# Weight conversions of the second block started one unit earlier, unread products in every early pause, and shorter memsets

## The chip, the cores and the metric

The kernel runs on one core of one Trainium2 chip. The metric is the device time of one execution in microseconds (us). Five queues of instructions work side by side: TensorE (PE, matmuls; its weight loads are shown as PEld), VectorE (DVE), ScalarE (ACT), GpSimd (POOL), and SyncE (SP), which here only issues DMAs. TensorE runs at one of two clocks, 1.2 or 2.4 GHz; the profile shows the granted clock as a share of the higher one, 0.50 or 1.00.

## What is computed

Causal attention with a decay, and two feed-forward blocks behind it. Cut to what matters:

```python
scores = scale * np.matmul(q, k.transpose(0, 1, 3, 2))        # (4, 8, 576, 576)
cum = np.cumsum(np.log(np.clip(f, 0.0001, 1.0)), axis=-1)
scores = np.where(causal, -1e9, scores + cum[..., :, None] - cum[..., None, :])
attn = softmax(scores)                                         # sum + 1e-09
x = np.matmul(attn, v)  -> (2304, 512)
h = x @ moe_w_in;  g = np.maximum(0.01 * h, h);  y = g @ moe_w_out           # d_ff 2048
out = (silu(y @ moe2_w_gate) * (y @ moe2_w_val)) @ moe2_w_out                # d_ff 1536
```

The weights arrive as 64-bit floating point numbers; the kernel turns them into 32-bit ones itself.

## The kernel before, in words

The sequence of 576 positions is worked on in units (b, u): four batches b = 0 to 3, and in each a unit u = 0 of 320 queries in three row tiles and a unit u = 1 of 256 queries in two. So with 8 heads the attention of a unit is 24 or 16 steps. Unit (0, 0) is done in 32-bit matmuls (`attention_f32`), all others with operands split in two 16-bit parts: for each head the scores (PE), a custom VectorE operation with the decay and the mask, the exponential (ACT), the split into two halves (ACT and DVE, into `ph_ring`), and a DMA transpose that turns the probabilities for the product with V. Beside the attention of one unit run the matmuls of the first block (`moe_h`, `moe_y`) of the unit before it (`along`, line 1273). The second block runs after all attention, with its weights prepared by `prep_gv` and `prep_o2`.

The weights of the second block pass through `place` (line 879): a DMA of 512 KB of raw words into `stage`, three integer operations on VectorE that make 32-bit numbers (`to_f32`, line 538), a pass of ScalarE that finds the largest magnitude, and a DMA of 256 KB back to DRAM (`gate_val_dram`, or `out_dram` written from `wi_bytes` or `wo_bytes`; the name stands for the tensor `out2_dram`). There are 36 places: 24 for the gate and value weights (`stage_gv`) and 12 for the output weights (`stage_o2`). `along` takes one of them at each step t with t % every == 0; `every` is 2 in batches 2 and 3 and 0 in batch 1.

Nothing is issued as written. A planner (`Plan`) records every operation, works out dependences and due times, and simulates five queues in twelve rounds of list scheduling; the order with the shortest plan is emitted. So an edit in one place shifts the order elsewhere too. An operation recorded while `nc.behind` is set may not be planned ahead of the one it names; before, this holds for DMAs alone.

`emit` (line 353) also puts unread products into pauses of PE: 128x512 matmuls of zeroes out of `mask` into the last PSUM bank, `banks[-1]` (line 371), as many as fit in 0.9 of the planned pause at 216 ns each. Line 368 stops this at 30 us of the plan: `min(op.start, WARM)`.

In `decay` (line 578) VectorE forms the cumulated logarithms that the first heads need, while GpSimd writes constants: ones into four pieces of `wo_bytes`, and zeroes into the whole of the two buffers of `ph_ring` (six memsets of 128x768).

Of the kernel before, what the change touches and what calls it, by code (L numbers as in the profile page):

```python
# [20 lines left out]
P = 128  # L21
# [55 lines left out]
SLACK = 50e3  # L77
FILL = 0.9
FIRST = 2.5e3
WARM = 30e3  # L80
URG = 8


class Plan:
# [44 lines left out]
    def new(self, eng):  # L129
        op = Op()  # L130
        op.eng, op.calls, op.dur, op.succ, op.npred = eng, [], 0.0, [], 0
        op.reads, op.writes, op.bytes = [], [], 0
        op.urgent = self.urgent
        op.behind = None if self.urgent or eng != "SP" else self.behind
        return op

    def begin(self):
# [215 lines left out]
    def emit(self, rounds=12):  # L353
        self.link()
        self.dues()
        best = None
        for k in range(rounds):
            order = self.schedule(k == 0)
            end = max(op.end for op in order)
            if best is None or end < best[0]:  # L360
                best = (end, order, [(op.start, op.end) for op in self.ops])
            self.backward()
        for op, (a, b) in zip(self.ops, best[2]):
            op.start, op.end = a, b
        at = 0.0
        for op in best[1]:
            if op.eng == "PE":
                pause = min(op.start, WARM) - at + (FIRST if at == 0.0 else 0.0)
                for _ in range(int(max(0.0, pause) * FILL / (426.0 if at < COLD else 216.0))):
                    ps, w, x = self.filler  # L370
                    self.tensor.real.matmul(ps, lhsT=w, rhs=x, start=True, stop=True)
                at = op.end
            for fn, args, kw in op.calls:
                fn(*args, **kw)  # L374


class Ring:
# [5 lines left out]
    def next(self):  # L383
        self.n += 1
        return self.bufs[(self.n - 1) % len(self.bufs)]
# [21 lines left out]
def body(ctx, tc, qk, v, f, w_in, w_out, w_gate, w_val, w_out2, out):  # L407


    nc = Plan(tc.nc)  # L410
    B, H = qk.shape[:2]
# [6 lines left out]
    NF = DF // P  # L418
    NF2 = DF2 // P
# [3 lines left out]
    hw = P // 2  # L423


    UNITS = [(0, 320, (0, 1, 2)), (320, 256, (3, 4))]
    KEYS = [q0 + nq for q0, nq, _ in UNITS]
# [9 lines left out]
    NB2 = DF2 // FB2  # L437
# [32 lines left out]
    n = a_m.at  # L470
# [14 lines left out]
    NBK = [12, 18]  # L485
# [10 lines left out]
    n = KW[0][-1]  # L496
# [3 lines left out]
    n = 9 * P  # L500
# [77 lines left out]
    def decay():  # L578
        n0 = UNITS[0][1]
        scr = wo_t.t[:R, :]  # L580
        fr, one, cum = (scr[:, i * S:(i + 1) * S] for i in range(3))
        one = one[:, :n0]
# [15 lines left out]
        nc.gpsimd.partition_all_reduce(lib, lib, P, ABSMAX)  # L598
        nc.gpsimd.memset(mask, 0.0)
        nc.urgent = False  # L600

        nc.filler = (banks[-1], mask[:, :P], mask[:, :4 * P])
        nc.gpsimd.affine_select(out=mask[:, 4 * P:], in_=mask[:, 4 * P:], pattern=[[-1, P + hw]],
                                compare_op=ALU.is_ge, fill=NEG, base=0, channel_multiplier=1)
        csf = scr[:, 3 * S:3 * S + 4 * W].rearrange("r (a s) -> r a s", a=4)
        cs = csf.bitcast(F32R)

        for x in ph_ring.bufs:
            for a in range(0, NBK[1] * P, 6 * P):
                nc.gpsimd.memset(x[:, a:a + 6 * P], 0.0)  # L610
        for u, (q0, nq, _) in enumerate(UNITS):
            col, _, qc, kc = COLS[u]
            nc.gpsimd.memset(csf[:, :2, col + kc:col + kc + KEYS[u]], 1.0)
            nc.gpsimd.memset(csf[:, 2:, col + qc:col + qc + nq], 1.0)
        nc.scalar.copy(out=cum[:, :n0], in_=c0)
        nc.vector.tensor_tensor_scan(out=cum[:, n0:], data0=one[:, :S - n0], data1=fr[:, n0:],
                                     initial=c0[:, n0 - 1:n0], op0=ALU.mult, op1=ALU.add)
        for u, (q0, nq, _) in enumerate(UNITS):
            col, wd, qc, kc = COLS[u]
            n = KEYS[u]  # L620
# [267 lines left out]
    def stage_o2():  # L888
        for a in range(NF2):
            place(words(w_out2, NF2)[:, a:a + 1, :, :], o2d[a], am_o2[:, a:a + 1])  # L890
            yield

    def stage_gv(n):

        fs = slice(n * FB2, (n + 1) * FB2)
        ch = RAW // FB2
        nr = NC // ch
        for m, (w, s, i) in enumerate(((w_gate, s_g, i_g), (w_val, s_v2, i_v2))):
            am = sm(nr, "ami")
            for x in range(nr):  # L900
                place(words(w, NC)[:, x * ch:(x + 1) * ch, fs, :], gvd[2 * n + m, :, x * RAW:(x + 1) * RAW], am[:, x:x + 1])
                yield
            m1 = sm(1, "m1")
            nc.vector.tensor_reduce(out=m1, in_=am, axis=AX.X, op=ALU.max)

            scale_f32(s[:, n:n + 1], i[:, n:n + 1], m1, 13, "i")
# [351 lines left out]
    def chain(*gens):  # L1258
        for g in gens:
            yield from g  # L1260
# [12 lines left out]
    def along(at, mo, total, every=0):  # L1273

        cost = [0.0, 0.0]
        full = H * sum(KW[at[1]])
        for t, w in enumerate(at[0]):
            if every and t % every == 0:
                step(gv_places)
            cost[0] += w / full  # L1280
            while cost[1] < cost[0]:
                r = next(mo, None)
                if r is None:
                    break
                cost[1] += r / total
        run(mo)
# [21 lines left out]
    prev = (1, 0)  # L1308
    todo = [(b, u) for b in range(1, B) for u in range(2)][1:]
    gv_places = chain(*(stage_gv(n) for n in range(NB2)), stage_o2())  # L1310
    for b, u in todo:
        gs = []
        along((attention(b, u), u), chain(moe_h(*prev, gs), moe_y(*prev, gs)),
              12.0 * 2 * NF * UNITS[prev[1]][1], 2 if b > 1 else 0)
        prev = (b, u)
    run(gv_places)
    gs = []
# [74 lines left out]
```

## Time and profile before

| | us |
|---|---|
| median of 3 runs | 951.02 |
| lowest, highest run | 949.59, 953.21 |
| the profiled execution | 951.74 |
| its span | 949.7 |
| PE busy in the span | 919.4 (97%) |
| DVE busy | 801.7 (84%) |
| ACT busy | 679.7 (72%) |
| POOL busy | 46.4 (5%) |

A busy share near 100% says only that matmuls were in flight: a matmul at half clock, or an unread product, counts as busy like any other. So the busy shares are read together with the granted clock, and the idle stretches of PE together with what released it. Time runs from the start of the span; between the span and the time of the execution lie 2.0 us.

### The profile page before, as it was taken

The numbers are of one execution on the slowest core, as the hardware profiler recorded it, in microseconds if no ns is written. First come the engines' busy times: TensorE is split into PE (matmuls) and PEld (weight loads), VectorE is DVE, ScalarE is ACT, GpSimd is POOL, SyncE is SP. The second block draws the span as 40 slices with busy tenths as digits, with TensorE's granted clock in tenths as the row PEclk, the third lists the DMA queues.
The fourth block names the chain that finished last, engine by engine and source line by source line (L and its number), as shares of the span: only waits on it lengthen the run. The fifth ranks groups of instructions, "written<-read, shape, count | busy, mean of one in ns | idle before, by whom it ended". The sixth has DMA issues, their size and how long they took to land.

```text
span 949.7 us, 25231 instructions
## 1 busy us (share of the span) xinstructions
PE 919.4 (97%) x9951; PEld 787.6 (83%) x9951; DVE 801.7 (84%) x2052; ACT 679.7 (72%) x1673; POOL 46.4 (5%) x118
## 2 busy tenths in 40 slices
PE   8899999999998999998999999899999999999998
PEld 5567778877787777786777899889999999999997
DVE  7878999996789989889878999999587786958685
ACT  5857889996678988788786868767466574746462
POOL 5200000000000000100000000000000000000000
PEclk8979999999999999999999999999999999999999
DMA  7657995575899999989957243011001010010001
GB/s 225 186 162 232 265 204 148 122 173 136 169 236 237 272 255 249 260 226 320 273 112 185 97 131 116 23 52 41 24 24 36 13 35 24 25 35 2 25 2 46
DMA packets 162199, 128.22 MB, mean 135 GB/s; under 512 B 117232, under 2 KB 130544, under 8 KB 162048
## 3 DMA queue, kind: packets, MB, share of 16 engines
q1 hardware_dynamic: 162080, 126.61, 50.8%
q8 instruction: 78, 1.28, 0.5%
q14 instruction: 41, 0.34, 0.1%
HBM read 78.60 MB, written 19.63 MB: 103 GB/s over the span
## 4 chain that ended last, share of the span: by engine, by line
PE 56%; DVE 26%; DMA 9%; ACT 5%; issue 3%; SPq 1%; POOL 0%; DVEq 0%; ACTq 0%; POOLq 0%
PE bank L374 55%; DVE att_bytes L374 6%; DVE wi_bytes L374 5%; DVE g_bytes L374 4%; DVE stage L374 4%; DMA att_bytes<-att_bytes 4%; DVE wo_bytes L374 3%; ACT att_bytes L374 1%; DVE smalls L374 1%; DMA stage<-in_moe_w_val_dram 1%; DVE ta L374 1%; DVE tb L374 1%; DVE moe_bytes L374 1%; SPq L374 1%; ACT stage L374 1%
## 5 line engine op out<-in xcount | busy, mean ns | idle before, releaser
L374 PEld LDWEIGHTS <-att_bytes 128*128 128x128 f16 (+1 forms) x4062 | 234.8, 100 | 25.6 <-issue 21.2
L374 PE MATMUL bank<-g_bytes,wo_bytes 128*128 128x256 f16 (+2 forms) x1472 | 209.2, 297 | 0.8 <-DVE wo_bytes L374 0.5
L374 PE MATMUL bank<-moe_bytes,wi_bytes 128*128 128x256 f16 (+2 forms) x1472 | 205.8, 299 | 0.0
L374 ACT ACTIVATE att_bytes<-att_bytes,smalls 128x576 f32<-128x576 f32 (+12 forms) x308 | 173.9, 591 | 39.5 <-DVE smalls L374 31.3
L374 PEld LDWEIGHTS <-wi_bytes 128*128 128x128 f16 x2100 | 173.5, 98 | 32.9 <-issue 0.4
L374 PEld LDWEIGHTS <-wo_bytes 128*128 128x128 f16 x1344 | 127.0, 98 | 33.7 <-issue 2.9
L374 DVE TENSOR_TENSOR wi_bytes<-bank,wi_bytes 128x256 f32<-128x256 f32 x270 | 109.3, 419 | 42.4 <-PE bank L374 41.2
L374 PEld LDWEIGHTS <-g_bytes 128*128 128x128 f16 x1620 | 125.8, 98 | 11.6 <-issue 2.7
L374 ACT ACTIVATE wi_bytes<-wi_bytes,smalls 128x256 f32<-128x256 f32 (+2 forms) x129 | 69.9, 555 | 46.7 <-DVE wi_bytes L374 45.3
L374 PE MATMUL bank<-wi_bytes,att_bytes 128*128 128x128 f16 x1680 | 98.7, 219 | 0.7 <-DVE wi_bytes L374 0.7
L374 DVE SCALAR_TENSOR_TENSOR att_bytes<-att_bytes,smalls 128x576 f16<-128x576 f32 (+5 forms) x148 | 86.2, 615 | 5.6 <-ACT att_bytes L374 5.5
L374 PE MATMUL bank<-stage,att_bytes 128*128 128x128 f16 (+1 forms) x1389 | 86.7, 221 | 2.6 <-DVE wi_bytes L374 2.4
L374 DVE CUSTOM_DVE_ANT_0 att_bytes<-bank,att_bytes 128x320 f32<-128x320 f32 (+5 forms) x160 | 67.8, 443 | 14.5 <-PE bank L374 14.0
L374 ACT COPY wi_bytes<-bank 128x256 f32<-128x256 f32 x108 | 38.3, 364 | 55.6 <-PE bank L374 50.2
L374 PE MATMUL bank<-tb 68*128 68x256 f32 (+3 forms) x168 | 62.3, 381 | 3.6 <-ACT att_bytes L374 2.2
L374 PE MATMUL bank<-att_bytes 128*64 128x256 f16 (+3 forms) x804 | 48.5, 257 | 12.2 <-DMA att_bytes<-att_bytes 9.9
L374 POOL PARTITION_ALL_REDUCE smalls<-smalls x47 | 24.2, 518 | 691.5 <-DVE smalls L374 689.7
L374 DVE TENSOR_TENSOR g_bytes<-moe_bytes,g_bytes 128x320 f16<-128x320 f32 (+1 forms) x80 | 45.1, 567 | 14.0 <-ACT g_bytes L374 13.5
L374 ACT ACTIVATE wi_bytes<-wo_bytes 128x256 bf16<-128x256 f32 x108 | 44.0, 410 | 17.9 <-DVE wo_bytes L374 17.8
L374 PE MATMUL bank<-wo_bytes,g_bytes 128*128 128x256 f16 x432 | 54.9, 273 | 0.0
L374 PE MATMUL bank<-ta 128*128 128x256 f32 (+3 forms) x168 | 51.2, 315 | 0.0
L374 ACT ACTIVATE moe_bytes<-bank 128x320 f32<-128x320 f32 (+1 forms) x80 | 39.3, 492 | 11.4 <-PE bank L374 10.4
(123 smaller groups left out, 1425.7 us busy)
## 6 DMA issues: line engine op xcount, KB each, us to landing
stage<-in_moe_w_out_dram SPq DMA_DIRECT2D x28, 512.0 KB
att_bytes<-in_qk_dram SPq DMA_DIRECT2D x32, 416.0 KB
stage<-in_moe_w_in_dram SPq DMA_DIRECT2D x16, 512.0 KB
att_bytes<-in_qk_dram SPq DMA_DIRECT2D x24, 320.0 KB
stage<-in_moe_w_gate_dram SPq DMA_DIRECT2D x12, 512.0 KB
stage<-in_moe_w_val_dram SPq DMA_DIRECT2D x12, 512.0 KB
stage<-gate_val_dram SPq DMA_DIRECT2D x12, 512.0 KB
ta<-y_dram SPq DMA_DIRECT2D x18, 256.0 KB
```

What stands on the lines that cost most here:

```text
L374: fn(*args, **kw)
```

## The change

Four edits. The places of the second block start one unit earlier, in unit (1, 1), at an unchanged rate: 36 places over 72 steps is one in two steps (`rate`), so that they end after 16 of the 24 steps of unit (3, 0); before they began in (2, 0) and ended in (3, 1). The unread products are put into every planned pause until the first real product that writes the last bank, not only up to 30 us. The zeroes for `ph_ring` are written only to the halves of four blocks that no later operation writes before they are read. The ones in `wo_bytes` are written by ScalarE, as copies, and not ahead of the first scan of `decay`.

```diff
-WARM = 30e3
-        op.behind = None if self.urgent or eng != "SP" else self.behind
+        op.behind = None if self.urgent and eng == "SP" else self.behind
...
-        at = 0.0
+        at, bank = 0.0, self.filler[0].tensor.name
         for op in best[1]:
             if op.eng == "PE":
-                pause = min(op.start, WARM) - at + (FIRST if at == 0.0 else 0.0)
+                if bank in (w[0] for w in op.writes):
+                    bank = None
+                pause = op.start - at + (FIRST if at == 0.0 else 0.0) if bank else 0.0
...
+        scan = next(o for o in reversed(nc.ops) if o.eng == "DVE")
...
         for x in ph_ring.bufs:
-            for a in range(0, NBK[1] * P, 6 * P):
-                nc.gpsimd.memset(x[:, a:a + 6 * P], 0.0)
+            for i in (3, 8):
+                nc.gpsimd.memset(x.rearrange("p (n k) -> p n k", k=P)[:, i::9, hw:], 0.0)
+        nc.behind = scan
         for u, (q0, nq, _) in enumerate(UNITS):
             col, _, qc, kc = COLS[u]
-            nc.gpsimd.memset(csf[:, :2, col + kc:col + kc + KEYS[u]], 1.0)
-            nc.gpsimd.memset(csf[:, 2:, col + qc:col + qc + nq], 1.0)
+            for a, c, n in ((0, kc, KEYS[u]), (2, qc, nq)):
+                x = csf[:, a:a + 2, col + c:col + c + n]
+                nc.scalar.copy(out=x, in_=one[:, :1].unsqueeze(2).to_broadcast(x.shape))
+        nc.behind = None
...
-            if every and t % every == 0:
+            for _ in range(int((t + 1) * every) - int(t * every)):
                 step(gv_places)
...
+    rate = (4 * NB2 + NF2) / (sum(H * len(UNITS[u][2]) for _, u in todo) - 24)
     for b, u in todo:
...
-              12.0 * 2 * NF * UNITS[prev[1]][1], 2 if b > 1 else 0)
+              12.0 * 2 * NF * UNITS[prev[1]][1], rate)
```

In the changed file the unread products stand on line 372 and all other instructions on line 375, where before they stand on 371 and 374.

**ScalarE in `decay`.** The rows after the first copy on ScalarE. Before:

```order
L374 COPY wo_bytes<-wo_bytes 32x320
L374 ACTIVATE wo_bytes<-wo_bytes 32x320
L374 ACTIVATE wo_bytes<-wo_bytes 32x256
L374 ACTIVATE wo_bytes<-wo_bytes 32x320
L374 ACTIVATE wo_bytes<-wo_bytes 32x256
L374 ACTIVATE att_bytes,smalls<-att_bytes,smalls 128x320
```

With the change:

```order
L375 COPY wo_bytes<-wo_bytes 32x320
L375 COPY wo_bytes<-wo_bytes 32x2x576
L375 COPY wo_bytes<-wo_bytes 32x2x320 x2
L375 COPY wo_bytes<-wo_bytes 32x2x256
L375 ACTIVATE wo_bytes<-wo_bytes 32x320 x2
L375 ACTIVATE att_bytes,smalls<-att_bytes,smalls 128x320
```

Four copies now stand ahead of the first exponential (128x320); two of the smaller activations have moved behind the first nine exponentials. In the same place GpSimd's list has lost four memsets of `wo_bytes`, and its six memsets of 128x768 have become four of 128x2x64.

**PE at the end of `attention_f32`.** The scores of the last head (from `att_bytes` alone) and the diagonal products that turn its probabilities (`g_bytes,att_bytes`). Before:

```order
L374 MATMUL bank_68<-att_bytes 128x192
L374 MATMUL bank_69<-att_bytes 128x320
L374 MATMUL bank_67<-att_bytes 128x64
L374 MATMUL bank_73<-g_bytes,att_bytes 128x128 x2
L374 MATMUL bank_73<-g_bytes,att_bytes 64x128
L374 MATMUL bank_72<-g_bytes,att_bytes 128x128
```

With the change:

```order
L375 MATMUL bank_69<-att_bytes 128x320
L372 LDWEIGHTS att_bytes
L372 MATMUL bank_74<-att_bytes 128x512
...
L375 MATMUL bank_73<-g_bytes,att_bytes 128x128 x2
L375 MATMUL bank_73<-g_bytes,att_bytes 64x128
L375 MATMUL bank_71<-g_bytes,att_bytes 64x128
```

Sixteen unread products (the two rows on line 372, sixteen times) now stand between the last scores and the diagonal products; before, none. In the whole program there are 63 of them instead of 41; four stand ahead of the first product of the first block, the rest in other pauses of `attention_f32`.

**SP at the end of unit (3, 0).** The last DMA transposes of the unit (128x12x128), and the raw loads of the output weights (`in_moe_w_out_dram`). Before:

```order
L374 DMA_TRANSPOSE att_bytes<-att_bytes 128x12x128
L374 DMA stage<-in_moe_w_out_dram 128x1024
L374 DMA att_bytes<-in_qk_dram 128x832
L374 DMA_TRANSPOSE att_bytes<-att_bytes 128x12x128
L374 DMA tb_84<-cum_dram 4x832
L374 DMA out_dram<-wo_bytes 128x512
L374 DMA att_bytes<-in_qk_dram 128x832
L374 DMA stage<-in_moe_w_out_dram 128x1024
L374 DMA y_dram<-moe_bytes 128x2x256 x2
```

With the change:

```order
L375 DMA_TRANSPOSE att_bytes<-att_bytes 128x12x128
L375 DMA tb_84<-cum_dram 4x832
L375 DMA att_bytes<-in_qk_dram 128x832
L375 DMA tb_85<-cum_dram 4x832
L375 DMA_TRANSPOSE att_bytes<-att_bytes 128x12x128 x2
L375 DMA tb_84<-cum_dram 4x832
L375 DMA att_bytes<-in_qk_dram 128x832 x2
L375 DMA y_dram<-moe_bytes 128x2x256 x2
```

No raw load and no store of converted weights stands beside the last three transposes any more. In exchange, eight raw loads now stand among the eight transposes of unit (1, 1), where there were none.

## Rows read from the trace of the kernel before

**Rows 1.** The page: PE's granted clock in 40 slices, tenths.
```profile
PEclk8979999999999999999999999999999999999999
```

**Rows 2.** Windows: stretch, busy us of PE, PEld, DVE, ACT, POOL; clock; DMA share; GB/s.
```profile
12.00:19.00 7.00, 7.00 (x26) 4.83 (x25) 5.95 (x25) 4.50 (x21) 2.54 (x6) 0.51 0.94 293
48.00:58.00 10.00, 10.00 (x34) 6.62 (x35) 8.11 (x21) 5.11 (x16) 0.80 (x2) 0.50 0.61 176
450.40:455.10 4.70, 4.70 (x34) 3.73 (x34) 4.70 (x9) 4.49 (x11) 0.15 (x1) 0.50 1.07 411
```

**Rows 3.** Timeline, PE's idle time: start, us, operation, [idle before it, and its releaser].
```profile
11.06 1.40 PE L374 MATMUL bank<-att_bytes 66*128 66x320 f32 x6 [2.35 <-DVE smalls L374]
47.97 3.62 PE L374 MATMUL bank<-g_bytes,att_bytes 128*128 128x128 f32 x12 [3.37 <-POOL g_bytes L374]
450.40 1.76 PE L374 MATMUL bank<-att_bytes 128*64 128x64 f16 x23 [3.35 <-DMA att_bytes<-att_bytes]
617.76 0.83 PE L374 MATMUL bank<-stage,att_bytes 128*128 128x128 f16 x12 [1.90 <-DVE wi_bytes L374]
```

**Rows 4.** Groups by shape on DVE and POOL, 0 to 12 us: count | busy, mean ns.
```profile
L374 DVE TENSOR_SCALAR wo_bytes<-wo_bytes 32x320 fp32r<-32x320 f32 x1 | 2.6, 2623 | 0.3 <-ACT wo_bytes L374 0.3
L374 DVE TENSOR_SCALAR wo_bytes<-wo_bytes 32x576 fp32r<-32x576 f32 x1 | 1.1, 1059 | 0.0
L374 DVE TENSOR_SCALAR wo_bytes<-wo_bytes 32x576 f32<-32x576 f32 x1 | 0.5, 500 | 0.9 <-DMA wo_bytes<-in_f_dram 0.9
L374 POOL MEMSET att_bytes<- 128x768 f16 x6 | 4.6, 808 | 0.0
```

**Rows 5.** Timeline of ACT in the first 12 us.
```profile
3.34 0.68 ACT L374 ACTIVATE wo_bytes<-wo_bytes 32x576 f32<-32x576 f32 x1 [1.26 <-DVE wo_bytes L374]
5.45 0.44 ACT L374 COPY wo_bytes<-wo_bytes 32x320 f32<-32x320 f32 x1
9.96 0.47 ACT L374 ACTIVATE wo_bytes<-wo_bytes 32x320 fp32r<-32x320 f32 x1 [3.27 <-DVE wo_bytes L374]
11.04 0.56 ACT L374 ACTIVATE att_bytes<-att_bytes,smalls 128x320 f32<-128x320 f32 x1
```

**Rows 6.** Timeline of PE: diagonal products of the first heads.
```profile
14.70 3.56 PE L374 MATMUL bank<-g_bytes,att_bytes 128*128 128x128 f32 x12
```

**Rows 7.** Windows as in Rows 2: behind the second fall, to 200 us, and unit (1, 1).
```profile
48.00:62.00 14.00, 14.00 (x46) 9.27 (x47) 9.43 (x24) 7.13 (x20) 0.80 (x2) 0.57 0.61 181
80.00:200.00 120.00, 117.27 (x878) 93.92 (x877) 116.30 (x319) 108.41 (x256) 2.64 (x11) 1.00 0.79 196
200.00:260.00 60.00, 60.00 (x490) 44.56 (x490) 44.81 (x123) 44.98 (x97) 2.17 (x7) 1.00 0.64 141
```

**Rows 8.** The chain that ended last, pieces of DMA: start, us, transfer.
```profile
68.69 4.57 DMA stage<-in_moe_w_in_dram
443.09 7.27 DMA att_bytes<-att_bytes
```

**Rows 9.** The tile stage: count, duration ns min/median/max, first and last start.
```profile
L374 DVE TENSOR_SCALAR stage<-stage x68: 390/422/606, 14.9 to 482.8; 128x512 int32<-128x512 int32 x68
L374 DVE SCALAR_TENSOR_TENSOR stage<-stage x68: 651/689/769, 15.4 to 485.8; 128x512 int32<-128x512 int32 x68
L374 DVE SCALAR_TENSOR_TENSOR wi_bytes<-stage x34: 675/686/777, 17.2 to 468.2; 128x512 int32<-128x512 int32 x34
```

**Rows 10.** Timeline of PE: what waits at the ends of other units.
```profile
197.56 1.00 PE L374 MATMUL bank<-att_bytes 128*64 128x64 f16 x23 [1.08 <-DMA att_bytes<-att_bytes]
322.75 1.00 PE L374 MATMUL bank<-att_bytes 128*64 128x64 f16 x23 [1.58 <-DMA att_bytes<-att_bytes]
390.93 1.56 PE L374 MATMUL bank<-att_bytes 128*64 128x256 f16 x29 [1.30 <-DMA att_bytes<-att_bytes]
```

**Rows 11.** Timeline of SP around the end of unit (3, 0).
```profile
441.98 0.53 SPq L374 DMA_DIRECT2D stage<-in_moe_w_out_dram  x1
447.37 1.01 SPq L374 DMA_DIRECT2D stage<-in_moe_w_out_dram  x1
```

## The prediction

> **What bounds the kernel now.** I read PE first. It is busy for 919.4 of 949.7 us, so all its idle time together is 30 us, and no change of order can be worth more than that, except through the clock. So the second view is the granted clock: in 40 slices it is under 90% in the first and the third only [rows 1]. Finer windows show three stretches at half clock: 12 to 19 us (0.51), 48 to 58 us (0.50) and 450.4 to 455.1 us (0.50), with PE busy throughout [rows 2]. Work done at half clock takes twice its time, so these three cost about 3.4, 5.0 and 2.35 us. The third view is PE's idle time and its releasers: in front of each of these stretches PE had waited 2.35, 3.37 and 3.35 us, while the longest wait that no fall followed is 1.90 us [rows 3]. The first wait ends on VectorE, the second on GpSimd, the third on a DMA transpose. These three pauses and what they do to the clock are 9.07 + 10.75 = 19.8 us; the change touches all three. Behind the second fall VectorE is the late engine: from 80 to 200 us it is busy for 116.3 of 120 us, PE for 117.3 [rows 7]. So there is hardly slack there to lose a gain in, nor to find another.
>
> **The first pause: memsets.** Before the first heads VectorE runs two TENSOR_SCALAR in 3.68 us, and the smaller one (320 columns) takes 2.62 us against 1.06 us for 576 columns; an earlier one of 576 columns took 0.50 us [rows 4]. What runs beside them is GpSimd's six memsets of 0.81 us, 4.6 us in all. With the change these are four memsets of a sixth of the size, and the four of `wo_bytes` are gone, so GpSimd should be done before VectorE comes to this pair. By the 0.50 us row the pair then takes 0.8 us (0.50, and 320/576 of it), at worst the 1.06 us that the larger one still took, twice: 2.1 us. VectorE is 2.9 (1.6) us earlier, and PE's wait of 2.35 us, which is for VectorE to read the first head's scores, goes, or shrinks to 0.75 us. Then the clock has no reason to fall at 12 us. Together that would be up to 2.35 + 3.4 = 5.75 us.
>
> The Trainium skill, "SBUF — State Buffer", section "SBUF: two separate sides", has a rule for this: VectorE (in a mode that takes both ports) and GpSimd share one pair of ports, whoever starts first holds it for a whole instruction, and the other blocks. By that rule each of the pair waits for one memset at most, 2 x 0.81 us; the change would then give back 1.6 us and not 2.9. The trace does not agree with it in size, since 2.62 us is longer than a memset and the 0.50 us row together.
>
> But the ones of `wo_bytes` are now ScalarE's, four copies of 1152, 640, 640 and 512 columns ahead of the first exponential. By the slope between 0.44 us for 320 columns and 0.68 us for 576 [rows 5] these are 1.2, 0.75, 0.75 and 0.6 us, 3.3 us. ScalarE is free at 5.89 us, ends the copies at 9.2, two activations of 0.47 us later stands at 10.1, and so starts its exponentials 0.9 us earlier than the 11.04 us of before, not 2.4. The cover of VectorE's and PE's gain is thus short: the first diagonal products need the exponentials. I count the 0.9 us, and that the diagonal products of the first heads take 1.8 us at full clock in place of 3.56 [rows 6], and the like of it once more, 0.65 us, for the scores between: 3.3 us. Bounds: 0.9 us (the clock falls all the same) and 5.75 us.
>
> **The second pause: unread products.** Sixteen of them at 0.22 us are 3.5 us in a pause of 3.37 us, and they hold the clock if the pause is where the plan has it. Then the stretch from 48 to 58 us runs at full clock: 5.0 us. VectorE can follow, being idle for 4.6 of the 14 us from 48 to 62 [rows 7], mostly in waits for PE. Their cost: 0.1 us of overrun and 0.9 us for the four ahead of the first block, if no pause is there. 4.0 us. Bounds: 5.0 us, and a loss of 1.0 us if the pause has moved.
>
> What is late next are the raw loads of the first block's weights, whose landing stands in the chain at 68.69 us with 4.57 us [rows 8]. They are issued when VectorE frees a buffer of `stage`, so they move with it; I keep all 7.3 us for the likeliest case and price their loss as a rival.
>
> **The conversions.** A place costs VectorE 0.42 + 0.69 + 0.69 = 1.80 us [rows 9], 512 KB in and 256 KB out; ScalarE's pass and SP's two issues move with it. 36 places stay 36 places. What changes is what they stand beside. At the end of unit (3, 0) the last transpose is issued at 443.09 us, between raw loads at 441.98 and 447.37 [rows 11], and lands 7.27 us later [rows 8]; PE waits 3.35 us for it and then works 4.7 us at half clock. With the change no raw load stands there. Left is what the end of a unit without conversions shows, 1.08 us [rows 10]. 3.35 + 2.35 - 1.08 = 4.6 us gained; bounds 0 (the transposes are late anyway) and 5.7.
>
> In exchange eight places come into unit (1, 1). There PE is not idle at all, and VectorE for 60 - 44.8 = 15.2 us [rows 7]; eight places are 14.4 us, so they just fit. The end of (1, 1) will look like the end of a unit with conversions: 1.58 and 1.30 us of waiting, without a fall [rows 10]. I take 1.5 us, after the second, which is the same kind of unit (the 1.30 us, and 0.2 us within it); bounds 0 and 5.7 us (it goes as at 450 us).
>
> **Sum.** 3.3 + 4.0 + 4.6 - 1.5 = 10.4 us. From the profiled execution of 951.74 us that is 941.3; the median of the runs is 0.7 us lower, so 940.6 us against 951.02.
>
> **Rivals.**
> A, the start is given back. VectorE and the raw loads bound 60 to 200 us, and the loads land when DRAM delivers them. For it: the chain goes through them and through VectorE, not PE. Against it: from 48 to 62 us the DMA share is only 0.61 [rows 7]. Only the conversions stay: 951.0 - 3.1 = 947.9 us, within 0.5%.
> B, the change does not do what it says at the second pause: the sixteen products end before the real wait does, or stand ahead of it, and the clock falls as before. For it: the plan's pauses are a model's. Against it: plan and trace have the pause in the same place. 3.3 + 4.6 - 1.5 - 1.0 = 5.4 us: 945.6 us.
> C, slower. VectorE is full in (1, 1): 44.8 + 14.4 = 59.2 of 60 us. Then the probabilities of its four pairs of heads are split late, each pair's last transpose lands late among raw loads, and PE waits as at 450 us, 3.35 us and 2.35 us of half clock, 5.7 us each time. It decides from the third of these on: 4 are 22.8 us, 3 are 17.1, against 3.3 + 4.0 + 4.6 = 11.9 us gained. With three, 951.0 + 5.2 = 956.2 us. For it: VectorE's 15.2 us of idle time lie in waits, not in a block. Against it: units (2, 0) and (2, 1) carry the same rate, and each shows one such wait at its end, of 1.58 and 1.30 us, with no fall.
>
> **How the numbers follow.** The forecast gets 0.60, A 0.18, B 0.12, C 0.10. The predicted time is that of the forecast, 940.6 us. A measurement of this kernel can tell about 0.5%, 4.8 us, from no change. The range reaches down to 935.0 us (5.75 + 5.0 + 4.6 = 15.4 us with nothing lost in (1, 1) is 935.6) and up over B and A to 950.0 us; what is left out is C and the ends of the forecast. The forecast's own range is 935 to 946. Faster by over 0.5% (below 946.3): 0.71, being the forecast and most of B; within: 0.19; slower: 0.10.
>
> **What the changed profile would show.** Right: two TENSOR_SCALAR of `wo_bytes` near 0.3 and 0.5 us; no wait of PE over 2 us before 60 us, and a granted clock of 1.00 throughout; the diagonal products of 47.97 us some 3 us earlier; the wait at the end of (3, 0) near 1 us; VectorE nearly full from 195 to 255 us and PE's waits there under 2 us in all. Wrong: a stretch at 0.50 left between 40 and 60 us (B); the start earlier but the first product behind 197 us not (A); two or more waits of over 2 us in (1, 1) (C). The forecast falls altogether if the new order, which twelve rounds of planning make anew, has put a wait of over 2 us where none was before, since each brings its half clock with it.

## The result, and the profile after

The changed kernel takes 941.91 us (median of 7 runs, 938.83 to 946.57) against 951.02 us before: a ratio of 0.9908 with a 95% interval of 0.9881 to 0.9934, or 8.7 us (6.3 to 11.3). 940.6 us had been forecast, within 935 to 950. The profiled execution took 940.95 us, its span 939.2. The page, PE's row and the granted clock in 40 slices, to be held against [rows 1]:

```profile
span 939.2 us, 25235 instructions
PE 915.0 (97%) x9969; PEld 784.4 (84%) x9973; DVE 798.9 (85%) x2052; ACT 681.6 (73%) x1677; POOL 40.6 (4%) x112
PEclk9999999999999999999999999999999999999999
```

The three stretches of [rows 2], and those of [rows 7] that answer, in windows (stretch, its length, busy us and instructions of PE, PEld, DVE, ACT and POOL; granted clock; DMA share; GB/s):

```profile
12.00:19.00 7.00, 6.63 (x41) 4.54 (x41) 6.85 (x20) 6.10 (x27) 4.01 (x8) 1.00 1.07 266
48.00:58.00 10.00, 9.84 (x46) 6.69 (x46) 9.87 (x25) 8.56 (x22) 0.00 (x0) 1.00 0.47 140
450.40:455.10 4.70, 4.70 (x37) 3.40 (x35) 3.73 (x10) 4.48 (x12) 0.00 (x0) 1.00 0.99 188
80.00:200.00 120.00, 115.99 (x894) 93.28 (x893) 114.91 (x324) 106.67 (x252) 2.90 (x12) 1.00 0.83 192
200.00:260.00 60.00, 58.52 (x473) 42.89 (x472) 53.70 (x151) 46.31 (x108) 3.74 (x9) 1.00 0.91 208
```

All three falls are gone (0.51, 0.50 and 0.50 before), and the same 10 us from 48 on hold 46 matmuls (three of them unread) where 34 stood. One fall is new, too short to show in 40 slices: about 3 us at half clock from 607.7 us on, which cost 1.6 us (its window stands in the last section). What PE lost for it is in the last two rows: it waits 4.0 us between 80 and 200 us (2.7 before), and 1.5 between 200 and 260, where it had not waited at all. Its waits that answer to [rows 3] and [rows 10], and the new ones (timeline: start, us, operation, count, in brackets the idle time ahead and what ended it):

```profile
42.96 4.08 PE L375 MATMUL bank<-g_bytes,att_bytes 128*128 128x128 f32 x24 [1.23 <-POOL g_bytes L375]
127.36 1.56 PE L375 MATMUL bank<-att_bytes 128*64 128x256 f16 x29 [2.01 <-DMA att_bytes<-att_bytes]
261.75 1.56 PE L375 MATMUL bank<-att_bytes 128*64 128x256 f16 x29 [1.67 <-DMA att_bytes<-att_bytes]
307.61 0.36 PE L375 MATMUL bank<-tb 68*128 68x256 f32 x1 [2.11 <-DMA tb<-cum_dram]
441.93 0.44 PE L375 MATMUL bank<-tb 68*128 68x448 f32 x1 [0.83 <-issue]
444.38 1.03 PE L375 MATMUL bank<-att_bytes 128*64 128x64 f16 x24
606.71 0.83 PE L375 MATMUL bank<-stage,att_bytes 128*128 128x128 f16 x12 [1.90 <-DVE wi_bytes L375]
```

No wait stands near 11 us any more, and the second pause is down from 3.37 to 1.23 us. At the end of unit (3, 0) the wait of 3.35 us for the last transpose is gone altogether: the products that read it, at 444.38 us, wait for nothing. The 0.83 us at 441.93 stand ahead of another operation and end on nothing that the profile shows. The conversions (the tile `stage`, as in [rows 9]) now end with unit (3, 0)'s second third:

```profile
L375 DVE TENSOR_SCALAR stage<-stage x68: 378/422/515, 12.4 to 430.6; 128x512 int32<-128x512 int32 x68
```

**What PE loses, stretch by stretch.** For every profile I summed, over windows of 1 us, PE's idle time and the part of its busy time that half clock took (busy time, times one less the granted clock). What is left of the span is work at full clock: 906 to 908 us, and 5 to 7 us more with the unread products in all early pauses. All sums are from one execution each, and some of these lie at the edge of their kernel's times: a_nomem and a_norate are the fastest of ten and twelve, f_only, a_norate48 and after48 the slowest of eleven, six and six. So a row shows where an execution lost time; by how much two kernels differ is told by the medians.

| profile of | 0-65 | 65-200 | 200-430 | 430-455 | 455-625 | 625-end | work | span |
|---|---|---|---|---|---|---|---|---|
| before | 16.7 | 2.7 | 6.1 | 6.5 | 6.4 | 3.8 | 907.3 | 949.7 |
| changed | 3.6 | 4.0 | 8.6 | 0.8 | 5.6 | 3.3 | 913.3 | 939.2 |
| f_only | 7.0 | 3.1 | 5.6 | 6.8 | 10.1 | 3.1 | 912.7 | 948.4 |
| m_only | 12.1 | 1.5 | 7.8 | 7.8 | 7.8 | 4.3 | 906.1 | 947.4 |
| r_only | 17.3 | 2.3 | 11.0 | 0.8 | 6.3 | 3.8 | 908.1 | 949.5 |
| a_nofill | 12.4 | 2.0 | 11.2 | 0.5 | 6.7 | 3.1 | 906.8 | 942.8 |
| a_nomem | 3.7 | 2.3 | 9.3 | 1.1 | 4.7 | 3.1 | 912.9 | 937.0 |
| a_norate | 3.0 | 2.6 | 9.0 | 7.7 | 7.7 | 3.4 | 911.4 | 945.0 |
| a_norate_b | 2.6 | 3.7 | 9.9 | 6.0 | 8.8 | 4.2 | 912.7 | 947.7 |
| a_norate48 | 5.3 | 4.7 | 7.3 | 7.4 | 6.3 | 4.0 | 913.5 | 948.6 |
| after48 | 5.4 | 3.2 | 15.3 | 1.2 | 4.5 | 3.1 | 912.8 | 945.5 |
| a_spread | 3.2 | 4.9 | 4.9 | 2.6 | 11.5 | 3.7 | 912.8 | 943.5 |
| b_quarter | 15.3 | 4.7 | 3.4 | 5.9 | 7.0 | 3.8 | 906.2 | 946.1 |
| cs_only | 12.2 | 2.4 | 11.9 | 6.0 | 8.0 | 3.1 | 905.7 | 949.3 |

From before to the changed kernel: 13.1 us less at the start, less 6.0 us of unread work; 1.3 us more from 65 to 200; 2.5 more from 200 to 430; 5.7 less from 430 to 455; 1.3 less behind. That is 10.3 of the 10.5 us between the spans.

### The profile page after: what moved, and what is told of

Read it like the earlier page. It is cut to its first block, busy times and chain, and to the rows that moved or that the text cites. A ratio compares the mean times of both kernels' runs of the same rounds, so it can differ in the third digit from the quotient of the medians.

```text
span 939.2 us, 25235 instructions
## 1 busy us (share of the span) xinstructions
PE 915.0 (97%) x9969; PEld 784.4 (84%) x9973; DVE 798.9 (85%) x2052; ACT 681.6 (73%) x1677; POOL 40.6 (4%) x112
## 3 DMA queue, kind: packets, MB, share of 16 engines
q8 instruction: 78, 1.28, 0.6%
## 4 chain that ended last, share of the span: by engine, by line
PE 57%; DVE 25%; DMA 8%; ACT 5%; issue 3%; SPq 1%; POOL 1%; ACTq 0%; DVEq 0%; POOLq 0%
PE bank L375 56%; DVE att_bytes L375 6%; DVE wi_bytes L375 5%; DMA att_bytes<-att_bytes 4%; DVE stage L375 4%; DVE g_bytes L375 4%; DVE wo_bytes L375 2%; ACT att_bytes L375 2%; DVE smalls L375 1%; PE bank L372 1%; DMA stage<-in_moe_w_gate_dram 1%; DVE tb L375 1%; DVE moe_bytes L375 1%; DVE ta L375 1%; SPq L375 1%
## 5 line engine op out<-in xcount | busy, mean ns | idle before, releaser
L375 PE MATMUL bank<-moe_bytes,wi_bytes 128*128 128x256 f16 (+2 forms) x1472 | 202.7, 297 | 1.2 <-DVE moe_bytes L375 1.1
L375 ACT ACTIVATE att_bytes<-att_bytes,smalls 128x320 f32<-128x320 f32 (+11 forms) x308 | 174.2, 591 | 37.3 <-DVE smalls L375 23.7
L375 DVE CUSTOM_DVE_ANT_0 att_bytes<-bank,att_bytes 128x320 f32<-128x320 f32 (+6 forms) x160 | 67.8, 443 | 9.4 <-PE bank L375 9.2
L375 DVE TENSOR_TENSOR g_bytes<-moe_bytes,g_bytes 128x320 f16<-128x320 f32 (+1 forms) x80 | 45.0, 566 | 11.6 <-ACT g_bytes L375 11.2
L375 ACT CAST ta<-att_bytes 128x832 fp32r<-128x832 f32 (+1 forms) x56 | 45.2, 807 | 3.2 <-PE bank L375 2.7
```

## The experiments

Times of a kernel are medians; one execution differs from another of the same kernel by some 5 us either way, so a profile shows where time lies and the ratio says what an edit is worth. Where a gain in us is given, it is the ratio's distance from 1, times 950.9 us.

**Each edit alone, and all without one.** The edits were told apart by their pieces of the diff: f, the unread products; m, the short memsets with the ones of `wo_bytes` on ScalarE; r, the spread conversions. An m or an r gives the planner other work and so another order everywhere; f changes no order, since the unread products go in after the planning, and the instructions of DVE, ACT and SP are the same with and without it.

f_only, the kernel before with this alone:

```diff
-                pause = min(op.start, WARM) - at + (FIRST if at == 0.0 else 0.0)
+                if bank in (w[0] for w in op.writes):
+                    bank = None
+                pause = op.start - at + (FIRST if at == 0.0 else 0.0) if bank else 0.0
```

> The kernel before with the unread products in all early pauses alone. Theory (each term stands for itself): the first pause stays as in [rows 3], 2.35 us behind VectorE, and its fall to 0.51 from 12 to 19 us too; the fall from 48 to 58 us is gone, and the diagonal products of 47.97 us run at full clock. 4 to 5 us are gained: about 946.5 us, and the end of (3, 0) still shows 3.35 us and a fall. Rival (the gain is given back behind the pause, where VectorE is full from 80 to 200 us): the fall is gone, the first store of y_dram (140.0 us before) is under 2 us earlier, and the time is 950 us or over.

946.33 us, ratio 0.9955 (0.9932 to 0.9977): 4.3 us. Windows of its profile, the first fall and where the second was:

```profile
12.00:19.00 7.00, 7.00 (x26) 4.64 (x25) 6.22 (x26) 4.49 (x21) 2.53 (x6) 0.55 0.98 298
48.00:58.00 10.00, 10.00 (x53) 6.87 (x52) 9.88 (x25) 7.48 (x22) 0.95 (x3) 1.00 0.69 204
```

The first fall stays, behind a pause of 2.05 us, and the second is gone, as the theory had it. Of the 9.7 us that the start loses less, 5.4 are paid as unread work.

m_only, the memsets alone:

```diff
-            for a in range(0, NBK[1] * P, 6 * P):
-                nc.gpsimd.memset(x[:, a:a + 6 * P], 0.0)
+            for i in (3, 8):
+                nc.gpsimd.memset(x.rearrange("p (n k) -> p n k", k=P)[:, i::9, hw:], 0.0)
...
-            nc.gpsimd.memset(csf[:, :2, col + kc:col + kc + KEYS[u]], 1.0)
+                nc.scalar.copy(out=x, in_=one[:, :1].unsqueeze(2).to_broadcast(x.shape))
```

> The kernel before with the short memsets, and the ones of wo_bytes written by ScalarE, alone. Theory: the two TENSOR_SCALAR of wo_bytes take 0.7 us together and not 3.68, PE's first pause of 2.35 us and the fall behind it are gone, 3 to 4 us; the second pause of 3.4 us and its fall from 48 to 58 us stay, 3 us earlier: about 947.5 us. Rival (what is saved ahead of a second pause is lost in it, since it is the raw loads that end it): the second pause grows by as much, and the time is 950 to 951 us.

948.57 us, ratio 0.9970 (0.9951 to 0.9989): 2.9 us. Windows and the second pause of its profile:

```profile
12.00:19.00 7.00, 6.86 (x40) 4.65 (x40) 6.39 (x19) 6.15 (x27) 3.60 (x7) 1.00 1.05 304
40.00:54.00 14.00, 12.45 (x45) 8.34 (x46) 9.61 (x24) 7.18 (x24) 3.49 (x7) 0.51 0.62 205
```

```profile
41.55 7.16 PE L374 MATMUL bank<-g_bytes,att_bytes 128*128 128x128 f32 x24 [3.25 <-POOL g_bytes L374]
```

The first fall is gone, the second pause comes 6.4 us earlier with all its length (3.25 us) and its fall. It did not grow; the theory holds, not the rival.

r_only, the conversions alone:

```diff
-            if every and t % every == 0:
+            for _ in range(int((t + 1) * every) - int(t * every)):
...
+    rate = (4 * NB2 + NF2) / (sum(H * len(UNITS[u][2]) for _, u in todo) - 24)
-              12.0 * 2 * NF * UNITS[prev[1]][1], 2 if b > 1 else 0)
+              12.0 * 2 * NF * UNITS[prev[1]][1], rate)
```

> The kernel before with the conversions of the second block spread from unit (1, 1) on, alone. Theory: both falls of the start stay; at the end of (3, 0) the wait of 3.35 us and the 2.35 us of half clock are gone, some 3 us come back as waits in (1, 1), and the time is 3 to 4 us lower, about 947.5 us. Rival 1 (the relief is lost again in unit (1, 1), or in a wait that sits elsewhere): within 1 us of 951. Rival 2 (part of what was gained at the start of the changed kernel is really owed to this edit, the sum of the parts being short without it): 945 us or less.

950.82 us, ratio 0.9995 (0.9976 to 1.0014): nothing, rival 1. The table shows where it goes. At 430 to 455 us 5.7 us are gained, just as in the changed kernel, but 200 to 430 us lose 4.9 us more than before. The main waits there end on DMAs, at the end of (1, 1) on a transpose and behind it on a load and a transpose:

```profile
257.95 1.56 PE L374 MATMUL bank<-att_bytes 128*64 128x256 f16 x29 [1.35 <-DMA att_bytes<-att_bytes]
312.40 0.36 PE L374 MATMUL bank<-tb 68*128 68x256 f32 x1 [2.11 <-DMA tb<-cum_dram]
396.18 2.88 PE L374 MATMUL bank<-att_bytes 128*64 128x256 f16 x29 [2.24 <-DMA att_bytes<-att_bytes]
```

The third brought half clock with it (its 29 matmuls take 2.88 us, those of 257.95 1.56). Not all of this is the price of the conversions. Up to 270 us r_only loses 2.3 us and the kernel before nothing; from 270 to 430 us it loses 8.6 us, and the seven profiles with the conversions and their loads as before lose 5.6 to 11.9 there (6.1 before).

a_nofill, the changed kernel without f: m and r together, `WARM` kept.

```diff
-                pause = op.start - at + (FIRST if at == 0.0 else 0.0) if bank else 0.0
+                pause = min(op.start, WARM) - at + (FIRST if at == 0.0 else 0.0)
```

> The changed kernel with unread products in the first 30 us only, as before the change. Theory: the pause that ended at 42.96 us in the changed kernel lies open for 3 to 5 us, the clock falls to half behind it for some 10 us, and the time is 4 to 5 us over the changed kernel's: about 946.5 us. Rival (the other two edits have taken away the reason for the pause, so that the unread products no longer matter): no stretch at half clock, 942 us.

945.14 us, ratio 0.9940 (0.9917 to 0.9964): 5.7 us. The second pause, and the clock behind it:

```profile
42.24 7.16 PE L374 MATMUL bank<-g_bytes,att_bytes 128*128 128x128 f32 x24 [4.78 <-POOL g_bytes L374]
```

```profile
40.00:54.00 14.00, 11.76 (x44) 7.90 (x45) 8.31 (x23) 6.21 (x21) 3.56 (x7) 0.52 0.55 179
```

This is the same order as the changed kernel's, with the pause left open: 4.78 us, and half clock to 53 us. The theory holds; in size it is 3.0 us over the changed kernel by the ratios, and not 4 to 5.

a_norate, f and m without r (the diff is that of r_only, backwards):

> The changed kernel with the conversions placed as before the change: short memsets and unread products alone. Theory: the start is that of the changed kernel, no fall before 65 us; the wait at the end of (3, 0) and its fall are back (4 to 6 us in the stretch 430 to 455 us, against 0.8), and the stretch 200 to 430 us loses 2 to 5 us less: 1 to 3 us over the changed kernel's, 943 to 945 us. Rival (the spreading is worth nothing in company either, as it was alone): 942 us.

951.51 us, ratio 0.9997 (0.9975 to 1.0018). Neither theory nor rival had this: two edits that gave 4.3 and 2.9 us each give nothing together. Its order is that of m_only, instruction by instruction, so it is also f on top of m, and there f gives nothing (951.51 us against 948.57). Its profile caught the fastest of 12 executions (946.86 us), so it can't say why; a_norate48 and a_norate_b below ask further.

a_nomem, f and r without m (the diff is that of m_only, backwards):

> The changed kernel with the long memsets of before: unread products and spread conversions. Theory: the first pause of 2 us and its fall of 3.4 us are back, the second has none, the end of (3, 0) has none; 941.9 + 2 to 3 us, about 944.5 us. Rival (the spreading gives nothing unless the start is undisturbed, as when it stood alone): that of the unread products alone, 946.5 us.

944.97 us, ratio 0.9937 (0.9914 to 0.9960): 6.0 us, as the theory has it in size. But in the profiled execution, which at 939.49 us was the fastest of ten, the first pause was 1.21 us and no fall followed, so that the mechanism named for the size did not show there. The pause ended where it does before, at 11.04 us against 11.06 [rows 3]; it was shorter because the eighteen unread products ahead of it, the same in both kernels, took longer. The first row is of the kernel before, the others of a_nomem:

```profile
1.57 5.87 PE L371 MATMUL bank<-att_bytes 128*128 128x512 bf16 x18 [1.57 <-POOL att_bytes L374]
```

```profile
1.57 7.01 PE L373 MATMUL bank<-att_bytes 128*128 128x512 bf16 x18 [1.57 <-POOL att_bytes L376]
11.04 1.30 PE L376 MATMUL bank<-att_bytes 66*128 66x320 f32 x6 [1.21 <-DVE smalls L376]
```

In r_only's profile, of the same order but for f, the eighteen took 6.68 us, the pause was 1.55 us, and the fall came. So the first pause differs between executions of one start, and what taking it away is worth probably differs too. a_nomem also has two long waits from 200 to 430 us without a fall: one in (1, 1), which r brings, and one for which the kernel before waits 1.37 us and others without r up to 1.88:

```profile
250.13 1.56 PE L376 MATMUL bank<-att_bytes 128*64 128x256 f16 x29 [2.06 <-DMA att_bytes<-att_bytes]
305.23 0.36 PE L376 MATMUL bank<-tb 68*128 68x256 f32 x1 [2.39 <-DMA tb<-cum_dram]
```

**Why the end of (3, 0) was late: b_quarter.** The second block's raw loads are cut to a quarter, everything else stands in the same order.

```diff
-        nc.sync.dma_start(raw.rearrange("p (a x) -> p a x", a=src.shape[1]), src.rearrange("p a b t -> p a (b t)"))
+        full = raw.rearrange("p (a x) -> p a x", a=src.shape[1])
+        part = full if nc.behind is None or nc.second is None else full[:, :, :full.shape[2] // 4]
+        nc.sync.dma_start(part, src.rearrange("p a b t -> p a (b t)")[:, :, :part.shape[2]])
```

> The kernel before, in its own order, but each raw load of the second block's weights carries a quarter of its bytes (the other three quarters of these weights are not loaded: left out). VectorE's and PE's instructions are the same. Theory (the transposes at the end of (3, 0) land late because raw loads stand beside them): the transpose of [rows 8] lands in 3 to 4.5 us in place of 7.27, PE waits 1.1 us or less in place of 3.35, no fall follows, and the stretch from 430 to 455 us loses 1 to 2 us in place of 6.5; 946 to 948 us in all. Rival (VectorE has the probabilities ready late, or the transposes are late of themselves): the wait stays over 2.5 us and the fall comes.

947.55 us, ratio 0.9967 (0.9944 to 0.9990). The time fits the theory, the place does not. Rows of SP and PE around the end of (3, 0):

```profile
438.81 1.43 SPq L375 DMA_TRANSPOSE att_bytes<-att_bytes  x1
```

```profile
443.72 1.00 PE L375 MATMUL bank<-att_bytes 128*64 128x64 f16 x23 [0.80 <-DMA att_bytes<-att_bytes]
449.99 22.28 PE L375 MATMUL bank<-moe_bytes,wi_bytes 128*128 128x320 f16 x153 [3.69 <-ACT moe_bytes L375]
```

The last transpose lands 4.9 us after its issue (443.72 - 438.81), not 7.27 as in [rows 8], and the wait for it is 0.80 us. That is above the 3 to 4.5 us expected, but the raw loads did make it late. But 6 us on PE stands 3.69 us for ScalarE's `moe_bytes`, which neither theory had: the stretch still loses 5.9 us (6.5 before). In both profiles VectorE is busy for all but 0.2 us of 430 to 450 us. The transpose was only the first to be late; behind it ScalarE's result is late by as much. Taking the conversions away there, as r does, takes both waits; taking only the DMA bytes away takes one. That it is the conversions' work on VectorE and ScalarE that makes the second late is likely but not shown apart, since r also makes a new order. Most of what b_quarter gains lies between 200 and 430 us (3.4 us lost, 6.1 before).

**How far to spread: a_spread.** Over all 96 steps to the last unit's end, not 72:

```diff
-    rate = (4 * NB2 + NF2) / (sum(H * len(UNITS[u][2]) for _, u in todo) - 24)
+    rate = (4 * NB2 + NF2) / (sum(H * len(UNITS[u][2]) for _, u in todo))
```

> The changed kernel with the conversions spread over all 96 steps that are left, the last unit's 24 too (36/96 in a step in place of 36/72). Theory (what the spreading costs in 200 to 430 us goes by the number of conversions there): that stretch loses 1 to 2 us less than the 8.6 us of the changed kernel, while the end of (3, 0) gets raw loads at its side again, but fewer: 1 to 3 us there in place of 0.8; 940 to 943 us. Rival (any raw load beside the last transposes of (3, 0) brings the long wait and its fall): 5 us or more there, 945 us and over.

946.43 us, ratio 0.9957 (0.9936 to 0.9978): 4.1 us faster than before, some 4.5 slower than the changed kernel. The two stretches go the theory's way (200 to 430 us loses 4.9 us, 3.7 less than in the changed kernel where 1 to 2 were expected; 430 to 455 loses 2.6), the time goes as the rival had it, for a reason of neither: 455 to 625 us lose 11.5 us in place of 5.6, most of it ahead of the second block:

```profile
583.28 0.37 PE L375 MATMUL bank<-stage,att_bytes 128*128 128x128 f16 x2 [4.40 <-ACT stage L375]
```

```profile
L375 DVE TENSOR_SCALAR stage<-stage x68: 376/420/514, 12.1 to 498.7; 128x512 int32<-128x512 int32 x68
```

The conversions now end at 500 us and the wait is a new one; that it is they that push VectorE's and ScalarE's other work toward 583 us is likely, but not shown.

**Which memsets: cs_only.** The ones of `wo_bytes` to ScalarE, the six long memsets left on GpSimd.

> The kernel before with only the ones of wo_bytes moved to ScalarE; the six long memsets stay on GpSimd. Theory (the long memsets slow VectorE's pair): GpSimd's memsets start some 2.6 us earlier, about 3.7 us, and end by 8.5 us; the TENSOR_SCALAR that runs beside them takes over 1 us, one that runs behind them 0.3 to 0.5 us. Rival (it was the four memsets of wo_bytes, the same tile, that slowed the pair): 0.7 us for the pair though the long memsets run beside it.

Groups of VectorE by shape in its first 12 us, and the row of GpSimd's memsets, six small ones and the six long ones:

```profile
L374 DVE TENSOR_SCALAR wo_bytes<-wo_bytes 32x576 fp32r<-32x576 f32 x1 | 1.1, 1059 | 0.0
L374 DVE TENSOR_SCALAR wo_bytes<-wo_bytes 32x320 fp32r<-32x320 f32 x1 | 0.7, 692 | 0.3 <-ACT wo_bytes L374 0.3
```

```profile
2.36 5.92 POOL L374 MEMSET att_bytes<- 64x128 f32 x12
```

The memsets run to 8.28 us, beside the whole pair (5.92 to 7.60). Both operations are slower than in the changed kernel, where GpSimd runs nothing beside them:

```profile
L375 DVE TENSOR_SCALAR wo_bytes<-wo_bytes 32x576 fp32r<-32x576 f32 x1 | 0.4, 440 | 0.0
L375 DVE TENSOR_SCALAR wo_bytes<-wo_bytes 32x320 fp32r<-32x320 f32 x1 | 0.3, 315 | 0.3 <-ACT wo_bytes L375 0.3
```

by 0.62 and 0.38 us. So the long memsets cost about 1.0 us together, and the other 1.93 of the pair's 3.68 us went with the four memsets of `wo_bytes`: the 2.62 us of [rows 4] do not come back. The theory is right on 576 columns only (1.06 us); the rival has the larger share on its side, but its 0.7 us for the pair is out. The first pause is gone with the long memsets still there. The stretch behind it, and the first exponentials of cs_only and of m_only:

```profile
12.00:19.00 7.00, 6.79 (x39) 4.47 (x39) 6.61 (x20) 6.10 (x27) 3.79 (x7) 1.00 1.06 312
```

```profile
9.34 0.55 ACT L374 ACTIVATE att_bytes<-att_bytes,smalls 128x320 f32<-128x320 f32 x1
```

```profile
9.34 0.54 ACT L374 ACTIVATE att_bytes<-att_bytes,smalls 128x320 f32<-128x320 f32 x1
```

The exponentials start at the same time, and the first 65 us lose 12.2 us here and 12.1 in m_only. So in these profiles the start's gain of m comes with moving the ones to ScalarE; the shorter memsets add nothing to be seen. One execution, 951.30 us, says nothing of the time that cs_only is worth.

**What an order is worth: a_norate48, after48 and a_norate_b.** One constant of the planner makes it find another order of the same work:

```diff
-SLACK = 50e3
+SLACK = 48e3
```

> Short memsets and unread products without the spreading, as in the run that gave 951.5 us, but with one constant of the planner changed (slack 48 us for 50) so that it finds another order of the same work. Theory (the 951.5 us belongs to that one order: another order of the same work costs up to 5 us more or less, mostly by which waits a fall follows): 944 to 948 us, the sum of the two parts alone being 944. Rival (the two edits without the third give the start's gain back in any order, since VectorE with the conversions on it is the later engine up to 450 us): 950 to 952 us.

> The changed kernel with the same constant of the planner changed (slack 48 us for 50): another order of the same work. Theory (an order is worth up to 5 us either way): anywhere from 937 to 947 us, over 2 us from the 941.9 us of the changed kernel. Rival (the edits decide, the order within them does not): within 1.5 us of 941.9.

a_norate48 takes 945.58 us, ratio 0.9936 (0.9911 to 0.9961), where a_norate had 0.9997 (0.9975 to 1.0018): the same edits, 5.8 us apart, with intervals that do not meet. The theory holds. after48 takes 944.88 us, ratio 0.9920 (0.9896 to 0.9943), against 0.9908 (0.9881 to 0.9934): the medians are 3.0 us apart, as the theory has it, but by the ratios it is 1.1 us, too little to tell. So an order can cost 6 us, and need not. Nor is the order of a_norate slow by itself: m_only has it too, without the unread products, and is 2.9 us faster than the kernel before.

> A second profile of the short memsets and unread products without the spreading, whose profiled execution of 946.9 us was the fastest of twelve with a median of 951.5. Theory: the first 65 us are again without a fall, and some 5 us more than in that profile are lost between 200 and 625 us, in waits of PE for transposes and the falls behind them. Rival: the first 65 us vary, with a fall in this execution and none in that.

This execution took 949.50 us. PE's waits where that profile and this one agree, from the first and then the second:

```profile
381.00 2.88 PE L376 MATMUL bank<-att_bytes 128*64 128x256 f16 x29 [3.18 <-DMA att_bytes<-att_bytes]
442.13 1.54 PE L376 MATMUL bank<-att_bytes 128*64 128x64 f16 x23 [2.46 <-DMA att_bytes<-att_bytes]
```

```profile
383.39 2.40 PE L376 MATMUL bank<-att_bytes 128*64 128x256 f16 x29 [2.85 <-DMA att_bytes<-att_bytes]
444.93 1.41 PE L376 MATMUL bank<-att_bytes 128*64 128x64 f16 x23 [2.65 <-DMA att_bytes<-att_bytes]
```

The first 65 us are again without a fall (2.6 us lost), so it is not the start that varies. Between 200 and 625 us this execution loses 24.7 us, that one 24.4: the 5 us looked for there are not, and the 2.7 us between the two are spread thin. Against the kernel before, the second profile has 14.1 us less lost at the start, 5.4 us more of unread work, and 7.1 us more lost behind 65 us, in many waits of 0.5 to 2.9 us. In this order the start's gain is mostly given back; why just here stays open.

## Why the prediction was right, point by point

**The bound.** PE's idle time and the granted clock were the right two views. Of the 10.5 us between the spans, PE's idle time gave 6.1 (30.3 us to 24.2) and half clock 10.4 (12.1 us to 1.7), and 6.0 us went back into unread work. Two readings of the kernel before were too small: over all of its length the second fall cost 6.0 us (5.0 by the window from 48 to 58 us), the third 2.7 (2.35).

**The start, 3.3 + 4.0 = 7.3 us.** Measured in the traces 7.1 (13.1 less 6.0). By the runs, m alone is worth 2.9 us and f alone 4.3. In f_only's trace the second pause (3.4 us) and its fall (6.0) are gone for 5.4 us of unread work, 4.0 us net, as forecast; of its parts the fall was worth 6.0 us and not 5.0, and the unread work beyond the pause cost 2.0 and not 1.0. f moves no other instruction, and yet its worth goes by what it is added to: 4.3 us (before), 5.5 (r), 3.0 (m and r) and -2.6 (m alone). m gave 2.9 (before), 5.2 (r), 2.7 (f and r) and, on f alone, -4.0 us in the order of a_norate and 1.8 in that of a_norate48. Those on other bases than the kernel before are differences of two ratios, good to some 3 us either way. So the two terms are borne out on the bases that the forecast had in mind, and not on every one.

**The memsets.** Right that the pair is faster (0.76 us by the two rows above, 0.8 forecast) and that ScalarE's copies take the cover away (its first exponential at 9.49 us, 10.1 forecast). The step that failed is the cause of the 2.62 us: the long memsets by themselves bring 1.0 us, as cs_only showed, and taking these away starts the first exponentials no earlier. The Trainium skill, "SBUF — State Buffer", section "SBUF: two separate sides", has VectorE, in a mode that takes both ports, and GpSimd lock a shared pair of ports for a whole instruction; by it, as the forecast worked out, each operation waits for at most one memset, 0.81 us. The trace of cs_only agrees (0.62 and 0.38 us). That of the kernel before does not: one operation there took 2.3 us longer than in the changed kernel. 1.93 us of that are gone in cs_only, with the memsets of `wo_bytes`; how these brought them is open.

**The end of (3, 0), 4.6 us.** The relief was 5.7 us in the changed kernel, and 5.3 to 6.0 in the other four whose conversions end before it; the forecast had left 1.08 us of waiting for the transpose, and none is left. The forecast put the whole on raw loads beside the transpose; b_quarter shows that they are only one part of the mechanism, and that without them the stretch loses almost as much, in a wait for ScalarE.

**The cost of the conversions in (1, 1), 1.5 us: the mis-sized term.** The wait at the end of (1, 1) is as forecast, 1.67 us, but it is not the only one there: from 200 to 270 us the changed kernel loses 3.1 us and the kernel before none. The table's column 200-430, split at 270 us, shows how far the cost reaches:

| profiles | 200-270 | 270-430 |
|---|---|---|
| conversions from (1, 1), ended in (3, 0): changed, r_only, a_nofill, a_nomem, after48 | 2.3 to 6.3 (changed 3.1) | 5.4 to 9.0 (changed 5.4) |
| conversions as before: before, f_only, m_only, cs_only, a_norate, a_norate_b, a_norate48 | 0.0 to 1.5 (before 0.0) | 5.6 to 11.9 (before 6.1) |

Up to 270 us the two groups stand apart; behind it they do not, and what a kernel loses there goes by its order. VectorE was not what filled up (53.7 of 60 us, 59.2 forecast); the waits end on DMAs, with a share of 0.91 where it had been 0.64. That this share is what makes them late is likely, but was not tested here. The net of r, 3.1 us by the forecast, came out at 0.5 (alone), 1.7 (on f), 2.8 (on m) and 1.5 us (on f and m, in the orders of the constant 48), and at 8.4 over a_norate. Again these are good to some 3 us: only the first is plainly below the forecast, and only the last plainly above. That the total was still met is in part luck: relief and cost were both too small by 1 to 2 us, and what was lost between 65 and 200 us (1.3 us more than before) was made up behind 455 us.

**The rivals.** A (start given back) is not what the changed kernel does. In a_norate most of the start's gain is lost again, but not where A had it: from 65 to 200 us its two profiles lose 2.6 and 3.7 us, 2.7 before. B is out: 1.00 from 48 to 58 us. C is out: no wait of over 2 us in (1, 1). What the forecast named as its own end, a new order with a wait of over 2 us, did come (2.01 us at 127.36, 2.11 at 307.61), and no fall followed. That was luck as far as the forecast goes, which took it that each such wait brings its fall; in after48, the same edits in another order, waits of 2.42 and 3.04 us brought theirs.

## What to carry to other kernels

Where a planner makes the order anew, time the same edit in a second order before giving it a share of the gain: here two orders of one set of edits stood 5.8 us apart, more than each edit alone was worth. To ask what an unread product or any filler is worth, add it behind the planning, so that nothing else moves, and count its own busy time. And before calling one late transfer the cause of a wait, see whether the engines beside it are idle there: with VectorE full, making the transfer early only handed the wait to the next operation. And take apart an edit that does two things: of m, moving the ones did the work at the start, and the shorter memsets did none that PE's losses show.

## What the runs showed of the hardware

A wait's length does not say whether the clock falls. In the profile of the kernel before each wait of over 2 us had its fall. But after waits of 2.95 us (m_only) and 3.05 us (a_spread) the clock stayed at 1.00, and the matmuls behind them took their 1.56 us:

```profile
383.51 1.56 PE L374 MATMUL bank<-att_bytes 128*64 128x256 f16 x29 [2.95 <-DMA att_bytes<-att_bytes]
```

```profile
127.20 1.56 PE L375 MATMUL bank<-att_bytes 128*64 128x256 f16 x29 [3.05 <-DMA att_bytes<-att_bytes]
```

while after waits of 1.78 us (a_norate48) and of 0.90 and 1.90 us close together (the changed kernel) it fell, to 0.50 for about 3 us. The first of these, and the stretch of the second in windows:

```profile
41.78 2.40 PE L376 MATMUL bank<-g_bytes,att_bytes 128*128 128x128 f32 x12 [1.78 <-POOL g_bytes L376]
```

```profile
604.00:612.00 8.00, 5.79 (x63) 5.28 (x63) 7.91 (x18) 4.93 (x12) 0.00 (x0) 0.79 0.26 66
```

The kernel before had 1.28 and 1.90 us at the same place, the second in [rows 3], with no fall:

```profile
615.03 0.83 PE L374 MATMUL bank<-stage,g_bytes 128*128 128x128 f16 x12 [1.28 <-DVE wi_bytes L374]
```

That profile is the exception: in ten others that show this pair of waits, 0.90 to 1.28 and then 1.90 us, the clock fell each time, the changed kernel's among them. So the forecast's reading that a wait of 1.90 us brings no fall held for one execution only. A fall costs anything from 1.4 us (b_quarter, at 449 us) to 7.4 by how long it lasts: the second pause's took 6.0 us in the profile before, 7.4 in r_only, and 1.7 in a_norate48, where unread products followed.
